# The last two rows of an output projection's weights loaded and multiplied in column halves, with the last half copied out of PSUM by two engines

## The chip, the cores and the metric

One core of one Trainium2 chip. The metric is the device time of one execution in microseconds (us), the median of several executions. The span of a profile is about 1.8 us shorter than the measured time of the same execution.

PE is TensorE, PEld its weight loads, DVE is VectorE, ACT is ScalarE, SP is SyncE. "q" after a name (SPq, ACTq) is that engine's sequencer, which issues DMAs. "Landing" is the moment when all 16 DMA engines that share a transfer have counted up its semaphore.

## The reference, cut to what matters

Grouped-query attention over a cache, followed by an output projection:

```
B, Sq, D = 32, 4, 1024;  Hq, Hkv, Sk, Dh = 32, 4, 2048, 128       # bf16
q = x @ wq ;  p = softmax(q k^T / sqrt(Dh)) ;  o = p v
y = o.transpose(0, 2, 1, 3).reshape(B, Sq, Hq * Dh) @ wo          # wo is (4096, 1024)
```

Only the last product matters here. `y` has 128 rows (batch times query) and 1024 columns. It is summed over 32 slices u of 128 values each; slice u needs one "row" of wo, 128 x 1024 values, 256 KB.

## The kernel before

The kernel streams 67 MB of K, 67 MB of V and the weights (151 MB in all) through one SyncE queue. The 8.4 MB of wo come last. They arrive in pieces of 4, 2 or 1 rows, the last row in two column halves; for each row PE runs two matmuls of 512 columns with the same weights, into two PSUM banks. The end of the kernel, with cuts marked:

```python
    WO = (4, 4, 4, 4, 4, 4, 2, 2, 2, 1)          # rows of wo for each piece
    NA = 512
    COLS = ((0, 0, NA), (NA, NA, D))              # (place in PSUM, first column, last column)
    # ...
        pieces = [(sum(WO[:c]), m, 0, D) for c, m in enumerate(WO)] + [(Hq - 1, 1, 0, NA), (Hq - 1, 1, NA, D)]
        # ... one DMA on SyncE's queue for each piece ...
        def oproj(u):
            for j, (at, n0, n1) in enumerate(COLS):
                # matmul for j == 0 (loads the weights), _matmul_held for the others (keeps them)
                p.op("pe", mm, [("wo", piece), ("ot", B - 1)], ("op", j) if u == Hq - 1 else None)

        def oproj_out():
            p.op("act", lambda e: e.activation(y_sb[:, 0:NA], ps_s[:, 0:NA], ACT.Copy), [("op", 0)], ("oe", 0))
            p.op("dve", lambda e: e.tensor_copy(y_sb[:, NA:D], ps_s[:, NA:D]), [("op", 1)], ("oe", 1))
            for j, (eng, n0, n1) in enumerate((("act", 0, NA), ("sp", NA, D))):
                p.dma(eng, ...out_flat[:, n0:n1]..., [("oe", j)], ("out", j), f"s_o{j}")
        # ...
        for u in range(Hq):
            oproj(u)
        oproj_out()
```

The pieces at the end are thus rows 28 and 29 together (512 KB), row 30 (256 KB), then 31a and 31b, the first and second half of row 31 (128 KB each).

## Time and profile before

| what | value |
|---|---|
| time, median of 3 runs | 363.42 us (363.31 to 363.45) |
| span of the profiled execution (363.58 us, not one of the three) | 361.8 us |
| mean DMA rate over the span | 419 GB/s |
| landings of the last four pieces | 356.81, 357.43, 357.78, 358.10 us |
| last output issued, landed, end | 359.515, 361.34, 361.79 us |

Two parts of the kernel before's page: the share of time in which the DMA engines were busy, in 40 slices of the span (a digit is tenths, 9 is 90% or more), and the chain of waits that ended last.

```profile
DMA  8999999999999999999999999999999999999995
...
## 4 chain that ended last, share of the span: by engine, by line
DMA 7%; PE 4%; SPq 0%; DVE 0%; issue 0%
```

The DMA row is full from the second slice to the last but one: the loads bound this kernel, and no engine's work in the middle is on the path. What this change can win is in the tail: from the last byte in to the end. The chain gives too coarse a view of that, so here is the timeline of the kernel before from 356.8 us: start, duration, engine, line, operation, output and inputs, and in brackets the idle time before and what ended it.

```profile
356.85 0.33 PEld L418 LDWEIGHTS ps_s<-big,KT_sb 128*128 128x128 bf16 x2 [0.91 <-DMA big<-in_wo_dram]
356.86 0.39 PE L418 MATMUL ps_s<-big,KT_sb 128*128 128x512 bf16 x1 [0.21 <-DMA big<-in_wo_dram]
357.08 0.38 PE L16 MATMUL ps_s<-big,KT_sb 128*128 128x512 bf16 x1
357.30 0.38 PE L418 MATMUL ps_s<-big,KT_sb 128*128 128x512 bf16 x1
357.52 0.38 PE L16 MATMUL ps_s<-big,KT_sb 128*128 128x512 bf16 x1
...
357.73 0.38 PE L418 MATMUL ps_s<-big,KT_sb 128*128 128x512 bf16 x1
357.95 0.38 PE L16 MATMUL ps_s<-big,KT_sb 128*128 128x512 bf16 x1
...
358.16 0.38 PE L418 MATMUL ps_s<-big,KT_sb 128*128 128x512 bf16 x1
358.38 0.38 PE L16 MATMUL ps_s<-big,KT_sb 128*128 128x512 bf16 x1
358.58 0.60 ACT L427 ACTIVATE P_sb<-ps_s 128x512 bf16<-128x512 f32 x1 [16.24 <-PE ps_s L418]
358.80 0.69 DVE L428 CAST P_sb<-ps_s 128x512 bf16<-128x512 f32 x1 [16.12 <-PE ps_s L16]
359.21 0.37 ACTq L430 DMA_DIRECT2D out_dram<-P_sb  x1
359.51 0.35 SPq L430 DMA_DIRECT2D out_dram<-P_sb  x1
```

Read it against the landings. PE waits for the 512 KB piece (landed 356.81), is let go at 356.86, and then runs eight matmuls one every 0.217 us without a gap. It is *behind* the loads: the last piece is there at 358.10, its matmul starts only at 358.38. After the last matmul VectorE copies 512 columns for 0.69 us, and only then is the second output issued. From the last landing to that issue, 1.42 us pass. ScalarE's copy and output, 0.2 us and more ahead, end nothing.

### The profile page before, as it was taken

The page shows a single profiled execution, that of the slowest core. Times are in us where ns is not written, and L with a number is a line of the kernel's source. Part 1 is how long each engine was busy: PE and PEld are TensorE (multiplying, and loading weights), DVE is VectorE, ACT ScalarE, POOL GpSimd, SP SyncE. Part 2 cuts the span into 40 slices and gives each one's busy share as a digit, 9 for nine tenths or more (in the row PEclk, how much of TensorE's full clock was granted, in tenths as well). Part 3 has the DMA queues.
Part 4 walks back from the last instruction along what each step waited for, and adds up shares of the span by engine and source line. Part 5 has one row for each costly group of instructions (what it writes and reads, how often), then busy time and mean ns, then how long its engine had stood idle before and what let it go on. Part 6 is the DMA issues. An engine that isn't in the chain of part 4 may idle for free. (4 is left out here: it accounts for less than half of the span.)

```text
span 361.8 us, 6210 instructions
## 1 busy us (share of the span) xinstructions
PE 307.2 (85%) x2998; PEld 146.8 (41%) x2338; DVE 269.1 (74%) x170; ACT 102.7 (28%) x110; POOL 165.3 (46%) x262
## 2 busy tenths in 40 slices
PE   1988788999989999988999888888888889889896
PEld 1002000454445544444445444444333344449711
DVE  0018799999899898879998888888888888856500
ACT  1014222333333333333333333333322223333000
POOL 8002055355555555554455444445555554444000
PEclk9999999999999999999999999999999999999999
DMA  8999999999999999999999999999999999999995
GB/s 328 429 431 433 429 428 420 431 428 428 425 422 435 426 429 424 432 428 431 426 424 435 425 431 424 429 431 429 429 424 431 429 429 424 428 433 428 412 414 197
DMA packets 11963, 151.66 MB, mean 419 GB/s; under 512 B 1328, under 2 KB 1840, under 8 KB 2480
## 3 DMA queue, kind: packets, MB, share of 16 engines
q1 hardware_dynamic: 11808, 151.39, 98.7%
q8 instruction: 6, 0.10, 0.1%
q10 hardware_dynamic: 144, 0.13, 0.1%
q14 instruction: 5, 0.04, 0.0%
HBM read 151.26 MB, written 0.26 MB: 419 GB/s over the span
## 5 line engine op out<-in xcount | busy, mean ns | idle before, releaser
L327 DVE STREAM_TRANSPOSE KT_sb<-big 128x2048 f32<-128x2048 f32 x64 | 146.6, 2293 | 16.8 <-DMA big<-in_k_cache_dram 16.8
L353 ACT ACTIVATE P_sb<-ps_s,negmx 128x2048 bf16<-128x2048 f32 x32 | 82.0, 2564 | 185.0 <-DVE negmx L349 185.0
L16 PE MATMUL ps_s<-KT_sb,QD_sb 128*128 128x512 bf16 x384 | 103.7, 377 | 0.0
L384 POOL COPY PD_sb<-PT_sb 32x1024 f32<-32x1024 f32 x62 | 64.1, 1034 | 63.4 <-PE ps_r L393 60.6
L384 POOL COPY big<-PT_sb 32x1024 f32<-32x1024 f32 x61 | 63.0, 1034 | 59.1 <-PE ps_r L393 56.3
L349 DVE TENSOR_REDUCE negmx<-ps_s 128x1 f32<-128x2048 f32 x32 | 73.2, 2286 | 12.4 <-PE ps_s L16 10.9
L393 PE MATMUL ps_r<-big 128*128 128x128 bf16 x1024 | 59.8, 219 | 11.3 <-PEq L85 11.3
L393 PE MATMUL ps_r<-big,PD_sb 128*128 128x128 bf16 x1024 | 59.8, 219 | 9.9 <-PEq L85 9.9
L393 PEld LDWEIGHTS ps_r<-big 128*128 128x128 bf16 x1024 | 57.9, 98 | 22.1 <-issue 21.6
L393 PEld LDWEIGHTS ps_r<-big,PD_sb 128*128 128x128 bf16 x1024 | 58.0, 98 | 21.2 <-issue 20.7
L340 PE MATMUL ps_s<-KT_sb,QD_sb 128*128 128x512 bf16 x128 | 48.3, 377 | 18.3 <-PEq L85 18.3
L340 PEld LDWEIGHTS ps_s<-KT_sb,QD_sb 128*128 128x128 bf16 x128 | 12.3, 96 | 103.1 <-issue 103.1
L362 DVE STREAM_TRANSPOSE PT_sb<-P_sb 128x1024 f32<-128x1024 f32 x32 | 39.8, 1245 | 15.8 <-ACT P_sb L353 15.8
L317 POOL COPY QD_sb<-QT_sb 32x64 f32<-32x64 f32 x128 | 29.4, 229 | 46.1 <-DVE QT_sb L296 20.4
L16 PE MATMUL ps_r<-ident 128*128 128x384 bf16 x173 | 33.3, 325 | 0.0
L365 PEld LDWEIGHTS ps_r<-ssum,permf 128*128 128x128 f32 x64 | 11.9, 187 | 24.8 <-issue 23.1
L402 ACT ACTIVATE QT_sb<-ps_r,rinv 128x128 bf16<-128x128 f32 x32 | 11.7, 367 | 29.5 <-PE ps_r L393 27.3
L278 DVE TENSOR_SCALAR KT_sb<-ps_r 128x512 bf16<-128x512 f32 x2 | 1.3, 686 | 20.1 <-PE ps_r L262 20.1
L16 PE MATMUL ps_s<-big,KT_sb 128*128 128x512 bf16 x32 | 12.1, 379 | 1.2 <-DVE KT_sb L409 1.1
L428 DVE CAST P_sb<-ps_s 128x512 bf16<-128x512 f32 x1 | 0.7, 691 | 16.1 <-PE ps_s L16 16.1
L418 PE MATMUL ps_s<-big,KT_sb 128*128 128x512 bf16 x30 | 11.4, 381 | 1.4 <-DMA big<-in_wo_dram 1.4
L251 PE MATMUL ps_r<-ident 128*128 128x384 bf16 x32 | 10.3, 322 | 0.0
(41 smaller groups left out, 85.3 us busy)
## 6 DMA issues: line engine op xcount, KB each, us to landing
big<-in_k_cache_dram SPq DMA_DIRECT2D x32, 2048.0 KB, 18.6
big<-in_v_cache_dram SPq DMA_DIRECT2D x32, 2048.0 KB, 22.1
big<-in_wq_dram SPq DMA_DIRECT2D x4, 2048.0 KB, 14.0
big<-in_wo_dram SPq DMA_DIRECT2D x6, 1024.0 KB, 22.8
big<-in_wo_dram SPq DMA_DIRECT2D x3, 512.0 KB, 24.5
P_sb<-in_x_dram SPq DMA_DIRECT2D x1, 256.0 KB, 2.7
big<-in_wo_dram SPq DMA_DIRECT2D x1, 256.0 KB, 21.8
big<-in_wo_dram SPq DMA_DIRECT2D x2, 128.0 KB, 19.1
```

Of the source, the lines that this page charges most:

```text
L16: return eng.add_instruction(mybir.InstMatmult(name=nc.get_next_instruction_name(), engine=eng.engine, start_tensor_calc=start, stop_tenso ...
L317: p.op("pool", lambda e, s=src, d=dst: e.tensor_copy(d, s), waits if g == 0 else [("pt", i - 2)] * (g == 1 and i > 1), ("qd", i) if g == G ...
L327: p.op("dve", lambda e, s=src, d=dst: e.transpose(d, s), waits, ("kt", i, c), gives="t_kt" if c else None)
L340: mm = lambda e, a_=(out_, lhsT, rhs), f=first, l=last: e.matmul(a_[0], lhsT=a_[1], rhs=a_[2], start=f, stop=l, skip_group_check=True)
L349: p.op("dve", lambda e: e.tensor_reduce(negmx[:, i % 4:i % 4 + 1], ps_s[:, :], AX.X, ALU.max, negate=True), [("qk", i)], ("negmx", i))
L353: p.op("act", lambda e: e.activation(P_sb[:, :, :, :].rearrange("p t r w -> p t w r"), ps_s[:, :].rearrange("p (t w r) -> p t w r", w=2, r=R),
L362: p.op("dve", lambda e: e.transpose(dst, src), [("exp", i)], ("pt", i))
L365: p.op("pe", lambda e: e.matmul(ring[(i if i == L else i // 2 * 2) % 4][:, 510 + i % 2:511 + i % 2], lhsT=permf[:, :], rhs=ssum[:, i % 4:i ...
L384: p.op("dve" if i >= B - 2 and g < i - B + 4 else "pool", lambda e, s=src, d=dst: e.tensor_copy(d, s), [free] * (g == 0 or i >= B - 2) + [ ...
L393: p.op("pe", lambda e: e.matmul(buf[:, 0:Dh], lhsT=pd_of(i)[:, t // 2, :, :, :, t % 2].rearrange("p x g q -> p (x g q)"), rhs=big[:, slot_ ...
L402: p.op("act", lambda e: e.activation(dst, src, ACT.Copy, scale=rinv[:, i % 4:i % 4 + 1]), [("pv", i), ("rinv", i)], ("o", i))
L418: mm = lambda e, a=(out_, lhsT, rhs): e.matmul(a[0], lhsT=a[1], rhs=a[2], start=(u == 0), stop=(u == Hq - 1), skip_group_check=True)
```

## The change

The intent is to shorten that stretch in three ways:

- **S** (split): rows 28 and 29 become two pieces, so that PE isn't held for both.
- **H** (halves): rows 30 and 31 land, and are multiplied, as 30a, 31a, 30b, 31b. The first half of y is finished before the second halves are in, and can be copied meanwhile.
- **C** (copies): the second half of y lies in two PSUM banks (288 and 224 columns), to be copied by ScalarE and VectorE at once. VectorE copies the first half too. Both outputs are issued on SyncE's queue.

Two banks are taken so that the two engines don't read the same one: the Trainium skill, "PSUM — Partial Sum Buffer", section "PSUM bank collisions raise a hardware error", says that two engines on one bank and quadrant at once raise an error and mostly read wrong data.

The diff, cut to its core:

```diff
-    WO = (4, 4, 4, 4, 4, 4, 2, 2, 2, 1)
+    WO = (4, 4, 4, 4, 4, 4, 2, 2, 1, 1)
     NA = 512
-    COLS = ((0, 0, NA), (NA, NA, D))
+    NB = 800
+    COLS = ((0, 0, NA), (512, NA, NB), (1024, NB, D))
...
-... + [(Hq - 1, 1, 0, NA), (Hq - 1, 1, NA, D)]
+... + [(Hq - 2, 1, 0, NA), (Hq - 1, 1, 0, NA), (Hq - 2, 1, NA, D), (Hq - 1, 1, NA, D)]
...
-            p.op("act", ...y_sb[:, 0:NA]..., [("op", 0)], ("oe", 0))
-            p.op("dve", ...y_sb[:, NA:D]..., [("op", 1)], ("oe", 1))
-            for j, (eng, n0, n1) in enumerate((("act", 0, NA), ("sp", NA, D))):
-                p.dma(eng, ..., [("oe", j)], ...)
+            for j, eng in enumerate(("dve", "act", "dve")):
+                copy(eng, *COLS[j], j)
+            for j, (n0, n1, waits) in enumerate(((0, NA, (0,)), (NA, D, (1, 2)))):
+                p.dma("sp", ..., [("oe", i) for i in waits], ...)
...
-        for u in range(Hq):
-            oproj(u)
+        for u in range(Hq - 2):
+            oproj(u, (0, 1, 2))
+        for js in ((0,), (1, 2)):
+            for u in (Hq - 2, Hq - 1):
+                oproj(u, js)
```

More of the change, by code (lines that the diff above doesn't have):

```diff
@@ L217, in bass_standalone__gqa_block_cached__sampling_kernel @@
         wo_v = wo.rearrange("(h p e) n -> p h (e n)", p=128, e=4)
-        pieces = [(sum(WO[:c]), m, 0, D) for c, m in enumerate(WO)] + [(Hq - 1, 1, 0, NA), (Hq - 1, 1, NA, D)]
-        assert sum(WO) == Hq - 1
+        pieces = [(sum(WO[:c]), m, 0, D) for c, m in enumerate(WO)] + [(Hq - 2, 1, 0, NA), (Hq - 1, 1, 0, NA), (Hq - 2, 1, NA, D), (Hq - 1, 1, NA, D)]
+        assert sum(WO) == Hq - 2
         for c, (u, m, n0, n1) in enumerate(pieces):
@@ L412, in oT_of, with oproj @@
             return oT_sb[:, u // 4, u % 4 // 2, :, :, u % 2].rearrange("p b s -> p (b s)")
-        def oproj(u):
-            for j, (at, n0, n1) in enumerate(COLS):
+        def oproj(u, js):
+            for j in js:
+                at, n0, n1 = COLS[j]
                 out_, lhsT, rhs = ps_s[:, at:at + n1 - n0], oT_of(u), wo_at(u, 1)[:, n0:n1]
-                if j == 0:
+                if j == js[0]:
                     mm = lambda e, a=(out_, lhsT, rhs): e.matmul(
@@ L426, in oproj_out, with copy @@
         def oproj_out():
-            p.op("act", lambda e: e.activation(y_sb[:, 0:NA], ps_s[:, 0:NA], ACT.Copy), [("op", 0)], ("oe", 0))
-            p.op("dve", lambda e: e.tensor_copy(y_sb[:, NA:D], ps_s[:, NA:D]), [("op", 1)], ("oe", 1))
-            for j, (eng, n0, n1) in enumerate((("act", 0, NA), ("sp", NA, D))):
-                p.dma(eng, lambda e, n0=n0, n1=n1: e.dma_start(out_flat[:, n0:n1], y_sb[:, n0:n1]),
-                      [("oe", j)], ("out", j), f"s_o{j}")
+            def copy(eng, at, n0, n1, j):
+                dst, src = y_sb[:, n0:n1], ps_s[:, at:at + n1 - n0]
+                if eng == "act":
+                    p.op(eng, lambda e: e.activation(dst, src, ACT.Copy), [("op", j)], ("oe", j))
+                else:
+                    p.op(eng, lambda e: e.tensor_copy(dst, src), [("op", j)], ("oe", j))
+            for j, eng in enumerate(("dve", "act", "dve")):
+                copy(eng, *COLS[j], j)
+            for j, (n0, n1, waits) in enumerate(((0, NA, (0,)), (NA, D, (1, 2)))):
+                p.dma("sp", lambda e, n0=n0, n1=n1: e.dma_start(out_flat[:, n0:n1], y_sb[:, n0:n1]),
+                      [("oe", i) for i in waits], ("out", j), f"s_o{j}")
         L = B - 1
```

## The prediction

> **What bounds the kernel now.** The loads: the page's DMA row is full in 38 of 40 slices, at a mean of 419 GB/s, and the chain of waits ends with wo loads and a short tail. The change touches only that tail; I read it from the timeline and the completion times of the loads.
>
> The last wo pieces complete at 356.81 us (rows 28 and 29, 512 KB), 357.43 (row 30), 357.78 (first half of row 31) and 358.10 (second half). Matmuls restart at 356.86 and run eight in a row, 0.217 us each, the last starting at 358.38. So PE, let go late by the 512 KB piece, ends 0.3 us later than the last data would force. ScalarE copies 512 columns (358.58, 0.60 us), VectorE the other 512 (358.80, 0.69 us). The last output issue starts at 359.51, its data lands at 361.34 (1.83 us later), and 0.45 us of closing work ends the span. From the last load to the last output issue: 1.41 us.
>
> **What the change does.**
> 1. Row 28 is there near 356.2 and row 29 near 356.85, so PE isn't held for both.
> 2. 30a, 31a, 30b, 31b land near 357.2, 357.5, 357.85, 358.17 (estimate). Bytes are the same; a 1 KB packet takes 46 ns against 84 ns for 2 KB, so row 30 in halves costs about 0.06 us.
> 3. The first half of y is finished after 31a, near 357.95: VectorE's 0.69 us copy runs 358.0 to 358.7, under the last loads and matmuls.
> 4. After 31b, matmuls of 288 and 224 columns start near 358.2 and 358.35 and end near 358.5 and 358.6. ScalarE: the Trainium skill, "ScalarE: Activation LUTs", section "What ACT_TABLE_LOAD costs", gives 186 ns plus 0.833 ns a column with immediate scale: 0.61 us for 512 (trace: 0.60), so an estimated 0.43 us for 288, to 358.95. VectorE: 0.69 us less 288 columns at 0.96 GHz ("VectorE: DVE Perf Modes", Specifications) is an estimated 0.39 us, from 358.7 (free of the first copy) to 359.1.
> 5. Both output issues are on SyncE, 0.35 us each: near 358.7 and 359.1. They don't collide.
> 6. A third matmul per row: 288 plus 224 columns stream as long as 512; PE's waits of 0.6 us at 350.5 and 353.0 absorb the rest. Two more load issues, made some 18 us before their landing, cost nothing.
>
> **Sum.** Last output issue from 359.51 to about 359.1: 0.4 us less, all on the critical path. Everything before 354 us is unchanged. Predicted 363.05 us, range 362.7 to 363.5; within 2% with 0.985, faster by over 2% 0.005, slower 0.01. The gain is 0.1%, above the spread of three runs (0.14 us).
>
> **What would show each step.** Timeline: PE's last waits are for the last halves; VectorE's first copy begins about 0.5 us before the last matmul ends; copies of about 0.43 and 0.39 us end near 358.95 and 359.1; second output issue near 359.1, landing 1.8 us later. The last load completes at 358.1 to 358.25.
>
> **What would make it wrong.** The last load landing after 358.3 (four small pieces with 1 KB rows); a longer landing of the second output, queued behind the first; a gap of over 0.1 us between VectorE's two copies; or slower restarts of PE when each half reloads its weights while data is awaited. Each is worth 0.1 to 0.3 us, so the gain could vanish, but not become 2%.

## The result, and the profile after

| | before | after |
|---|---|---|
| median of 6 runs | 363.43 us | 363.09 us |
| range of the 6 runs | 363.31 to 363.56 | 362.99 to 363.20 |
| ratio, 95% interval | | 0.9991 [0.9978, 1.0004] |

A ratio here is the mean time of one kernel's fast runs over the mean of the other's in the same rounds, so not quite the ratio of the medians quoted. At the 2% mark this is "the same". The interval just includes 1, but the two sets of six runs don't overlap, and a repetition below (five runs from 362.97 to 363.22 beside nine of before from 363.27 to 363.61) says the same: 0.34 us less by the medians here and 0.45 us there, about 0.1%.

The timeline of the kernel after, over the stretch shown above for before:

```profile
356.53 0.38 PE L420 MATMUL ps_s<-big,KT_sb 128*128 128x512 bf16 x1
356.74 0.38 PE L16 MATMUL ps_s<-big,KT_sb 128*128 128x288 bf16 x2
356.94 0.10 PEld L420 LDWEIGHTS ps_s<-big,KT_sb 128*128 128x128 bf16 x1 [0.41 <-DMA big<-in_wo_dram]
356.96 0.38 PE L420 MATMUL ps_s<-big,KT_sb 128*128 128x512 bf16 x1
...
357.40 0.84 PE L420 MATMUL ps_s<-big,KT_sb 128*128 128x512 bf16 x3
...
358.04 1.04 DVE L434 CAST P_sb<-ps_s 128x512 bf16<-128x512 f32 x2 [15.34 <-PE ps_s L420]
358.07 0.26 PE L16 MATMUL ps_s<-big,KT_sb 128*128 128x224 bf16 x1
358.25 0.10 PEld L420 LDWEIGHTS ps_s<-big,KT_sb 128*128 128x128 bf16 x1 [0.22 <-DMA big<-in_wo_dram]
358.26 0.30 PE L420 MATMUL ps_s<-big,KT_sb 128*128 128x288 bf16 x1
358.39 0.26 PE L16 MATMUL ps_s<-big,KT_sb 128*128 128x224 bf16 x1
358.59 0.41 ACT L432 ACTIVATE P_sb<-ps_s 128x288 bf16<-128x288 f32 x1 [16.23 <-PE ps_s L420]
358.76 0.82 SPq L439 DMA_DIRECT2D out_dram<-P_sb  x2
```

Instructions of the same line that follow each other are merged ("x2", named by the first one's shape). Singly, in the trace: VectorE copies 512 columns from 358.038 to 358.730 and 224 columns from 358.691 to 359.083; SyncE issues the two outputs at 358.757 and 359.225.

The landings of 28, 29, 30a, 31a, 30b, 31b are 356.24, 356.90, 357.21, 357.56, 357.89 and 358.21 us. PE is now level with the loads: it waits for 31a, 30b and 31b (30a's matmul still starts 0.19 us after its landing), and the last pair of matmuls starts at 358.26, 0.05 us after the last landing (before: 0.28 us). VectorE's long copy begins before that landing. The last issue is at 359.225 instead of 359.515, and its output lands at 360.96 instead of 361.34. From that landing to the end it is 0.45 us in both.

One point needs care. The *last load* doesn't land at the same time in each execution, and not in the order of the kernels: over the 14 traces it lies between 357.88 and 358.25 us. The spread is as large as the gain. So the experiments are judged by three distances inside one trace as well, which the loads' luck doesn't touch: from the last load's landing to the second output's issue, from that issue to its landing, and the sum of the two (the "tail").

### The profile page after: what moved, and what is told of

It reads as the page before. It is cut to its first block, busy times and chain, and to the rows that moved or that the text cites. A ratio compares the mean times of both kernels' runs of the same rounds, so it can differ in the third digit from the quotient of the medians.

```text
span 361.4 us, 6252 instructions
## 1 busy us (share of the span) xinstructions
PE 307.8 (85%) x3034; PEld 147.0 (41%) x2340; DVE 269.4 (75%) x171; ACT 102.6 (28%) x110; POOL 165.4 (46%) x262
## 5 line engine op out<-in xcount | busy, mean ns | idle before, releaser
L394 PE MATMUL ps_r<-big 128*128 128x128 bf16 x1024 | 59.8, 219 | 11.4 <-PEq L85 11.4
L420 PE MATMUL ps_s<-big,KT_sb 128*128 128x512 bf16 (+1 forms) x34 | 12.5, 375 | 2.0 <-DMA big<-in_wo_dram 1.2
L434 DVE CAST P_sb<-ps_s 128x512 bf16<-128x512 f32 (+1 forms) x2 | 1.0, 542 | 15.3 <-PE ps_s L420 15.3
L16 PE MATMUL ps_s<-big,KT_sb 128*128 128x224 bf16 (+1 forms) x62 | 12.0, 272 | 0.0
```

Source lines behind the costliest of these rows:

```text
L16: return eng.add_instruction(mybir.InstMatmult(name=nc.get_next_instruction_name(), engine=eng.engine, start_tensor_calc=start, stop_tenso ...
L394: p.op("pe", lambda e: e.matmul(buf[:, 0:Dh], lhsT=pd_of(i)[:, t // 2, :, :, :, t % 2].rearrange("p x g q -> p (x g q)"), rhs=big[:, slot_ ...
L420: mm = lambda e, a=(out_, lhsT, rhs): e.matmul(a[0], lhsT=a[1], rhs=a[2], start=(u == 0), stop=(u == Hq - 1), skip_group_check=True)
```

## The experiments

Twelve runs were made, in three sets of four, each set on one chip with its own runs of the kernel before. All gave correct results. Times are medians of five runs (before: three, after: six) beside the kernel before's of the same chip. Each distance is in us and from one trace; the column "last load to last copy's end" is part of the next one.

| run | parts | time (before, same chip) | last load | last load to last copy's end | last load to 2nd issue | 2nd issue to landing | tail |
|---|---|---|---|---|---|---|---|
| before | none | 363.42 | 358.10 | 1.39 | 1.42 | 1.82 | 3.24 |
| before_again | none | 363.34, one run (363.47) | 357.88 | 1.37 | 1.39 | 1.83 | 3.22 |
| s_only | S | 363.34 (363.53) | 357.98 | 1.17 | 1.20 | 1.82 | 3.02 |
| h_only | H | 363.43 (363.53) | 357.95 | 1.38 | 1.40 | 1.73 | 3.13 |
| c_only | C | 363.59 (363.53) | 358.00 | 1.45 | 1.65 | 1.73 | 3.38 |
| s_h | S, H | 363.25 (363.46) | 358.09 | 1.17 | 1.19 | 1.73 | 2.92 |
| s_c | S, C | 363.54 (363.46) | 357.93 | 1.25 | 1.45 | 1.74 | 3.19 |
| h_c | H, C | 363.39 (363.46) | 358.08 | 1.22 | 1.42 | 1.73 | 3.15 |
| after | S, H, C | 363.09 (363.43) | 358.21 | 0.87 | 1.01 | 1.74 | 2.75 |
| all_again | S, H, C | 363.08 (363.53) | 358.22 | 0.87 | 1.03 | 1.74 | 2.77 |
| waits | all, waits exchanged | 363.27 (363.46) | 358.25 | 0.87 | 1.03 | 1.75 | 2.78 |
| act_out | all, 1st output on ScalarE | 362.90 (363.47) | 357.94 | 0.87 | 0.97 | 1.73 | 2.70 |
| act_first | all, copies exchanged | 363.04 (363.47) | 358.09 | 0.84 | 0.93 | 1.73 | 2.65 |
| shared | all, both halves by both | 362.93 (363.47) | 358.08 | 0.84 | 0.91 | 1.71 | 2.61 |

The 95% intervals of the ratios are about 0.0013 (0.5 us) to either side, so the times alone tell few of these kernels apart; the distances in the traces do, and repeat within 0.025 us where a kernel was traced twice. Below, "before" and "after" without a run's name are the means of their two traces up to the second issue, 1.405 and 1.02 us.

My theory was that the three parts give the whole gain only together. Rival 1: the gain is PE's earlier release (S) and nothing else. Rival 2: the parts add up, and the shorter last copy (C) is the main one.

### s_only

```diff
-    WO = (4, 4, 4, 4, 4, 4, 2, 2, 2, 1)
+    WO = (4, 4, 4, 4, 4, 4, 2, 2, 1, 1, 1)
```

> The kernel before with one part of the change: rows 28 and 29 of wo as two pieces of 256 KB; row order, banks, copies and outputs as before. Theory (three parts that only work together): PE gets row 28 near 356.25 us and is level with the loads again, so the last matmul ends near 358.56 instead of 358.77; the VectorE copy of 512 columns still takes 0.69 us after it, so the last output issue starts near 359.31 instead of 359.51: 0.20 us faster. Rival 1 (the gain is PE's earlier release and nothing else): the whole 0.35 us. Rival 2 (the gain is the shorter last copy, each part counts for itself): 0.

Measured: 0.19 us faster by the medians, 0.21 us less from last load to second issue. The end of the timeline of the kernel with S alone:

```profile
357.82 0.38 PE L418 MATMUL ps_s<-big,KT_sb 128*128 128x512 bf16 x1
358.04 0.38 PE L16 MATMUL ps_s<-big,KT_sb 128*128 128x512 bf16 x1
358.24 0.60 ACT L427 ACTIVATE P_sb<-ps_s 128x512 bf16<-128x512 f32 x1 [16.06 <-PE ps_s L418]
358.46 0.69 DVE L428 CAST P_sb<-ps_s 128x512 bf16<-128x512 f32 x1 [15.94 <-PE ps_s L16]
```

The last matmul starts 0.06 us after the last landing (357.98). The copy behind it is unchanged. Rival 1 falls: the release is worth about half.

### h_only

```diff
 (to the kernel after)
-    WO = (4, 4, 4, 4, 4, 4, 2, 2, 1, 1)
+    WO = (4, 4, 4, 4, 4, 4, 2, 2, 2)
 (and columns, copies and outputs as before; matmuls of halves (0,) and (1,))
```

> The kernel before with one part of the change: rows 30 and 31 as first halves, then second halves, both in the loads and in the matmuls; rows 28 and 29 still one 512 KB piece, each half copied whole (ScalarE 0.60 us, VectorE 0.69 us), outputs on two queues. Theory: PE is let go at 356.86 by the 512 KB piece and has eight matmuls to run, the last ending near 358.75 whatever their order, so ScalarE's copy starts 0.2 us earlier, which ends nothing, and VectorE's ends near 359.5: 0.0 us of gain (between -0.05 and +0.05). Rival 1: 0. Rival 2 (parts add up): about 0.1 us faster.

Measured: 0.10 us faster by the medians, which is more than I expected, though within the noise of times. The issue is where it was expected (1.40 us after the last load, before: 1.42 and 1.39), so the order alone gains nothing up to there. The rest of the tail is 0.1 us shorter: the output lands 1.73 us after its issue instead of 1.82. This was the first sign of something the prediction hadn't: in this kernel the first output is issued 0.52 us ahead of the second instead of 0.31.

### c_only

```diff
 (to the kernel after)
-    WO = (4, 4, 4, 4, 4, 4, 2, 2, 1, 1)
+    WO = (4, 4, 4, 4, 4, 4, 2, 2, 2, 1)
 (and pieces as before)
-        for u in range(Hq - 2):
-            oproj(u, (0, 1, 2))
-        for js in ((0,), (1, 2)): ...
+        for u in range(Hq):
+            oproj(u, (0, 1, 2))
```

> The kernel before with one part of the change: second half in two banks, first half copied by VectorE, then 288 columns by ScalarE and 224 by VectorE, both outputs on one queue; loads and row order as before. Theory: the first half is finished only two matmuls before the end, near 358.54, so VectorE copies 512 columns from 358.58 to 359.27 and 224 columns only after that, to 359.64, and the second issue starts near 359.75: 0.15 to 0.25 us SLOWER than before. Rival 1: 0. Rival 2 (the shorter last copy is the gain): about 0.3 us faster.

Measured: 0.06 us slower by the medians, 0.24 us more from last load to second issue (expected 0.15 to 0.25). The end of the timeline of the kernel with C alone:

```profile
358.26 0.38 PE L16 MATMUL ps_s<-big,KT_sb 128*128 128x288 bf16 x2
358.46 0.99 DVE L434 CAST P_sb<-ps_s 128x512 bf16<-128x512 f32 x2 [15.79 <-PE ps_s L420]
358.58 0.41 ACT L432 ACTIVATE P_sb<-ps_s 128x288 bf16<-128x288 f32 x1 [16.25 <-PE ps_s L16]
359.18 0.82 SPq L439 DMA_DIRECT2D out_dram<-P_sb  x2
```

VectorE's two copies, 0.69 and 0.38 us, stand in a row, the first starting 0.47 us after the last landing (358.00): without H the first half is finished only two short matmuls before the second. ScalarE is done at 358.99 and idles. But the copies explain the smaller part of the loss: the second one ends 1.45 us after the last load, 0.08 us later than in before, and the second issue starts only 0.20 us after that (in before 0.03). Both outputs are on SyncE here, and the run `waits` takes this up. Rival 2 falls: C alone, as it was built, lengthens the path. The quicker landing (1.73 us) gives part of the loss back, again.

### all_again

The kernel after, unchanged.

> The whole change once more, on the same chip as the three parts. Both theories: 0.3 to 0.4 us faster than before, last load near 358.2, VectorE's copies near 358.04 to 359.08.

Measured: 0.45 us faster by the medians; last load to second issue 1.03 us, in the first trace 1.01. Beside it, the three parts measured alone on this chip give 0.21 less, nothing and 0.24 more up to the second issue, in sum no gain (0.03 us *more*); together they give 0.39 less. The parts don't add up.

### s_h

```diff
 (to the kernel after: columns, copies and outputs as before)
-    COLS = ((0, 0, NA), (512, NA, NB), (1024, NB, D))
+    COLS = ((0, 0, NA), (NA, NA, D))
-        for js in ((0,), (1, 2)):
+        for js in ((0,), (1,)):
```

> The whole change without its copies: rows 28 and 29 as two pieces and rows 30 and 31 in halves, but the second half in one bank, first half copied by ScalarE (0.60 us), second by VectorE (0.69 us), outputs on two queues. Theory: the last load lands near 358.2, its 512-column matmul ends near 358.65, VectorE copies from 358.68 to 359.37, last output issue near 359.39: about 0.12 us faster than before, less than the split alone, since the last load comes 0.1 us later. Rival 1 (PE's release alone): 0.35 us faster.

Measured: 0.21 us faster. Up to the issue it is what S alone gives (1.19 and 1.20 us): halves without the divided copy leave VectorE's 0.69 us behind the last matmul. I had expected the last load to be 0.1 us later than before; it landed at 358.09 here, inside the spread.

### s_c

```diff
 (to the kernel after: row 30 whole, row 31 in halves)
-    WO = (4, 4, 4, 4, 4, 4, 2, 2, 1, 1)
+    WO = (4, 4, 4, 4, 4, 4, 2, 2, 1, 1, 1)
 (and pieces and row order as before)
```

> The whole change without the half order: rows 28 and 29 as two pieces and the three copies, but row 30 whole, then row 31 in halves. Theory: the first half ends near 358.32, when 31a has been multiplied, so VectorE copies it from 358.35 to 359.04 and its 224 columns from there to 359.4; second issue near 359.53: 0.0 to 0.1 us faster than before. Rival 1: 0.35 us faster. Rival 2 (the shorter last copy): 0.3 us faster.

Measured: 0.08 us slower by the medians, which is outside what I had expected, though within the noise; 1.45 us from last load to second issue. In the timeline of this kernel VectorE's first copy starts 0.26 us after the last landing (357.93); with H it starts before it.

```profile
357.77 0.38 PE L420 MATMUL ps_s<-big,KT_sb 128*128 128x512 bf16 x1
357.99 0.38 PE L16 MATMUL ps_s<-big,KT_sb 128*128 128x288 bf16 x2
358.19 0.99 DVE L434 CAST P_sb<-ps_s 128x512 bf16<-128x512 f32 x2 [15.62 <-PE ps_s L420]
```

### h_c

```diff
 (to the kernel after)
-    WO = (4, 4, 4, 4, 4, 4, 2, 2, 1, 1)
+    WO = (4, 4, 4, 4, 4, 4, 2, 2, 2)
```

> The whole change with rows 28 and 29 as one 512 KB piece. Theory: PE is let go near 356.87, the first half ends near 358.34, VectorE copies it until 359.07 and its 224 columns until 359.42, second issue near 359.56: 0.0 to 0.1 us faster than before. Rival 1: 0. Rival 2: 0.3 us faster.

Measured: 0.07 us faster; 1.42 us from last load to second issue, 0.40 more than with S. PE, let go late, finishes the first half late: VectorE's first copy starts at 358.316, 0.23 us after the last landing, where with S it starts 0.16 to 0.18 us before it, and all that follows is later with it.

```profile
358.32 0.99 DVE L434 CAST P_sb<-ps_s 128x512 bf16<-128x512 f32 x2 [15.66 <-PE ps_s L420]
358.66 0.41 ACT L432 ACTIVATE P_sb<-ps_s 128x288 bf16<-128x288 f32 x1 [16.34 <-PE ps_s L420]
359.04 0.82 SPq L439 DMA_DIRECT2D out_dram<-P_sb  x2
```

So S is worth 0.21 us alone and 0.40 beside the others; H nothing alone and 0.43 beside the others; C costs 0.24 alone and gains 0.17 beside the others (all up to the second issue). The reason is one chain: last landing of a *first half*, its matmuls, VectorE's copy of 0.69 us, and then both issues on SyncE. In all six traces that have C with both outputs on SyncE and VectorE copying first (c_only, s_c, h_c, after, all_again, waits) the second issue starts 0.494 to 0.496 us after the end of that *first* copy, when the copy of 224 columns has been done for 0.14 to 0.20 us. So what counts is when the first copy starts: 0.23 to 0.47 us after the last landing where S or H is missing, 0.16 to 0.18 us before it where both are there.

C is two things, the divided copy (with VectorE on the first half too) and the move of both outputs to SyncE. Up to the end of the last copy C costs only 0.08 us alone and gains 0.30 beside the others; the rest, 0.17 alone and 0.13 beside them, is lost between the last copy and the second issue. No run has the divided copy with its outputs on two queues but without S or H, so how much of C's loss alone is the copies' is read from these distances and not from an experiment.

### waits

```diff
-            for j, (n0, n1, waits) in enumerate(((0, NA, (0,)), (NA, D, (1, 2)))):
+            for j, (n0, n1, waits) in enumerate(((0, NA, (0,)), (NA, D, (2, 1)))):
```

> The whole change with the two waits of the second output issue named in the other order. In the trace of after, VectorE's copy ends at 359.083, a wait instruction of SyncE on VectorE's semaphore is seen at 359.156, and the issue starts at 359.225, 0.142 us after the copy; in the kernel before, with one wait, it started 0.024 us after the copy. Theory: if the wait that comes last stands on the issue itself, the issue starts near 359.12 and 0.1 us more is gained (0.45 us faster than before). Rival: the 0.1 us is due to the two issues in a row on SyncE (the first ends at 359.104), and the order changes nothing.

Measured: 363.27 us (five runs from 362.99 to 363.61, wider than the others), and no change in the trace: last load to second issue 1.03 us (all_again: 1.03). SyncE's standalone wait is now on ScalarE's semaphore, whose copy was done at 359.041, and yet is seen only at 359.209, just after SyncE's first issue ended at 359.157; the second issue follows at 359.278. My reason falls, the rival holds. In all seven traces with both outputs on SyncE whose copies would have allowed an earlier issue or nearly so (c_only, s_c, h_c, after, all_again, waits and, at 0.487, act_first) the second issue starts 0.467 to 0.487 us after the first. In the first six it is 0.467 to 0.469, though the copies had been done for 0.14 to 0.20 us. Either order leaves one wait instruction between the two issues: 0.12 us lie between the end of the first (0.35 us long) and the start of the second, where each of the first loads of wo, with no such instruction between, starts 0.04 to 0.06 us after the end of the one before. So part of the distance may be that wait; no run has two outputs in a row without it.

### before_again

The kernel before, one look.

> The kernel before, for a second trace of it. How far do the loads move from one execution to the next, and does the second output again land 1.83 us after its issue? In all six traces of the runs so far with 0.47 us or more between the two output issues the second landed 1.73 to 1.74 us after its issue; with 0.31 us (before, and the split alone) 1.83 us. Theory (outputs issued close to each other hold each other up): 1.83 us again, since the issues are again 0.31 us apart. From the last load's completion to the last landing: 3.24 us, within 0.05. The last load's completion itself: 357.95 to 358.15.

Measured: tail 3.22 us, second output 1.83 us after its issue with the issues again 0.309 us apart, as expected; the last load was at 357.88, a little earlier than I had allowed. (The quoted text counts six traces with the longer distance; there were eight then, with 1.73 to 1.75 us.)

### act_out

```diff
-                p.dma("sp", lambda e, n0=n0, n1=n1: ...
+                p.dma(("act", "sp")[j], lambda e, n0=n0, n1=n1: ...
```

> The whole change with its first output issued on ScalarE's queue, after ScalarE's own copy. In all runs with two outputs on SyncE the second issue starts 0.468 us after the first, whether its data was ready 0.04 or 0.14 us before; so SyncE's pace, not the copy of 224 columns, is the last link. Theory: without the first issue in front of it the second starts near 359.11 to 359.16 (copy ends 359.08), some 0.08 us earlier, but the first output now starts near 359.03, and two outputs less than 0.31 us apart land slower (1.83 us instead of 1.73): 0.0 us of difference from the whole change, within 0.05. Rival (the landing was longer because of two queues, not of the short distance): also 1.83 us. Rival 2 (the landing differs only by chance): 1.73 us, 0.08 us faster than the whole change.

Measured: 362.90 us, 0.57 below before on that chip; tail 2.70 us, 0.05 to 0.07 below the kernel after's two traces. The end of this kernel's timeline:

```profile
357.76 1.05 DVE L434 CAST P_sb<-ps_s 128x512 bf16<-128x512 f32 x2 [15.21 <-PE ps_s L420]
...
358.33 0.41 ACT L432 ACTIVATE P_sb<-ps_s 128x288 bf16<-128x288 f32 x1 [16.11 <-PE ps_s L420]
358.48 0.37 ACTq L439 DMA_DIRECT2D out_dram<-P_sb  x1
358.91 0.35 SPq L439 DMA_DIRECT2D out_dram<-P_sb  x1
```

(The quoted text has data ready 0.04 us before an issue; the traces show 0.14 to 0.20.) My expectation was wrong in one premise: I had put ScalarE's issue behind the end of its own copy. The trace shows the issue at 358.48 in the middle of the copy (358.33 to 358.74), as soon as VectorE's first copy was done. That agrees with the Trainium skill, "PSUM — Partial Sum Buffer", section "Engine vs sequencer instructions": the sequencer waits for earlier instructions to be dispatched, not to complete. So the two issues are 0.43 us apart, and the second output lands after 1.73 us although there are two queues. With h_only and s_h (also two queues, 1.73 us at 0.52 and 0.75 us apart) this rules out "two queues" as the reason for 1.82. Chance is ruled out as well: three traces at 0.309 us apart show 1.824 to 1.829, eleven at 0.427 and more show 1.707 to 1.753. That fits outputs holding each other up when close, but *why* is not shown; no run sets the distance alone. In the three close traces the second issue also starts 0.06 us before the first has ended, in the eleven others after its end, so the overlap of the issues is as good a candidate as the distance.

The second issue is 0.05 us nearer to the last load, all that freedom from SyncE's pace brings: it still starts 0.096 us after the last copy, with SyncE's wait instruction seen 0.03 us after that copy and the issue 0.07 us behind the wait (before, with one wait, 0.03 us in all). So the second wait seems to cost a little once the pace is out of the way. The small gain fits what the Trainium skill, "DMA: Bandwidth & Descriptors", section "Issuing engines are not separate DMA queues", says: issuing from several engines saves the sequencer's time only.

### act_first

```diff
-            for j, eng in enumerate(("dve", "act", "dve")):
+            for j, eng in enumerate(("act", "dve", "act")):
```

> The whole change with ScalarE and VectorE exchanged: ScalarE copies the first half (0.60 instead of 0.69 us), VectorE 288 columns and ScalarE 224 of the second. Theory: first copy from 358.04 to 358.64, first issue near 358.67, so SyncE may issue again from 359.14; VectorE 358.60 to 359.06, ScalarE 358.69 to 359.05; second issue near 359.14, landing 1.73 us later: from last load to last landing 2.66 us instead of 2.75, time 0.05 to 0.1 us below the whole change. Rival (the last copy is the last link, not SyncE's pace): 0.02 us.

Measured: tail 2.65 us, as expected (2.66); time 0.43 us below before, so not told apart from the kernel after by time. Here the copies end at 358.929 and 358.924 and the second issue starts at 359.017, 0.487 us after the first: the two limits have nearly met.

### shared

```diff
-    COLS = ((0, 0, NA), (512, NA, NB), (1024, NB, D))
+    NC = 256
+    COLS = ((0, 0, NC), (1536, NC, NA), (512, NA, NB), (1024, NB, D))
-            for j, eng in enumerate(("dve", "act", "dve")):
+            for j, eng in enumerate(("dve", "act", "dve", "act")):
 (outputs wait for copies 0 and 1, and for 2 and 3; four matmuls per row)
```

> The whole change with the first half in two banks too, 256 columns each: VectorE copies 256, then 288 columns, ScalarE 256, then 224; four matmuls per row. Theory: first copies end near 358.4, first issue near 358.5, second copies end near 359.06, second issue near 359.12 (now bound by the copies, no longer by SyncE), landing 1.73 us later: from last load to last landing about 2.65 us, some 0.1 us below the whole change. It must not lose time in the four matmuls per row, which stream the same 1024 columns.

Measured: 362.93 us, 0.54 below before; tail 2.61 us, the shortest of all. The end of its timeline:

```profile
358.26 0.26 PE L16 MATMUL ps_s<-big,KT_sb 128*128 128x224 bf16 x1
358.39 0.94 SPq L440 DMA_DIRECT2D out_dram<-P_sb  x2
358.46 0.46 DVE L435 CAST P_sb<-ps_s 128x288 bf16<-128x288 f32 x1 [0.23 <-PE ps_s L421]
358.56 0.36 ACT L433 ACTIVATE P_sb<-ps_s 128x224 bf16<-128x224 f32 x1 [0.26 <-PE ps_s L16]
```

The first issue begins before the last copies do, and both engines now wait for PE, not for themselves (the brackets name PE, with idle time before). The path is now: landing, two matmuls, one short copy on each engine, one issue. By time, the ranges of act_out and shared (362.87 to 362.95, and 362.89 to 363.12) lie below all runs of before on their chip (363.32 to 363.56); by the 2% mark both are still "the same". That they beat the kernel after is shown by the tails (0.05 to 0.15 us) and not by times, which come from different chips with last loads up to 0.3 us apart.

## Why the prediction was right, point by point

- **Bound by loads, only the tail moves.** Right. The spans differ by 0.38 us, and so do the landings of the last output; PE's waits for loads up to 353 us are the same (a 0.6 us wait ends at 353.02 before and 353.04 after).
- **Step 1, PE's release.** Right: rows 28 and 29 land at 356.24 and 356.90 (predicted 356.2 and 356.85). s_only shows 0.21 us for it, of the 0.3 us of lag that the prediction named.
- **Step 2, the halves' landings.** 357.21, 357.56, 357.89, 358.21 against 357.2, 357.5, 357.85, 358.17. That small packets cost 0.06 us is neither shown nor refuted: the last load lands at 358.10 on the mean of the nine traces with four halves and at 357.98 on that of the five others, which is the expected direction, but the ranges overlap and the spread over executions, 0.37 us, is larger.
- **Step 3, the first copy under the last loads.** Right, within 0.04 us (358.04 to 358.73), and by the runs with one or two of the parts the heart of the gain.
- **Step 4, sizes of the last copies.** ScalarE 288 columns 0.412 us (predicted 0.43), VectorE 224 columns 0.392 us (0.39), ending at 359.01 and 359.08 (358.95 and 359.1). The Trainium skill's formula for ScalarE was good within 0.02 us.
- **Step 5, "They don't collide".** Wrong. The first issue, at 358.757, ends at 359.104, and SyncE starts its next one 0.468 us after the first's start, at 359.225 rather than 359.1. The last link is SyncE's pace, led by the *first* copy, and not the copy of 224 columns, which was done 0.14 us earlier. The runs waits and act_out show it: exchanging the waits changes nothing, and taking the first issue off SyncE brings the second 0.05 us nearer.
- **Landing, "1.8 us later".** Off by 0.09 us to the other side: 1.74 us. I took the duration from the kernel before, where the other output had been issued 0.31 us earlier. The prediction had named a *longer* landing behind the first output as a risk; it became shorter.
- **Step 6, costs of a third matmul and two more issues.** Right in the cost: 288 and 224 columns stream in the time of 512 (c_only: 0.219 us for the pair, 0.216 for 512). Wrong in "some 18 us before their landing": the last two issues took 6.3 and 2.1 us and started 17.4 and 11.4 us before their landing, which was still early enough.
- **The sum.** 0.4 us, where the medians show 0.34 and the traces 0.38. The two errors after the copies, 0.12 and 0.09 us, have opposite signs and nearly cancel; that is luck, and the total was better than its terms. That it was the *parts together* that mattered, and that C by itself would lose time, the prediction did not say, but the same arithmetic gave it for the experiments.

## What to carry to other kernels

In a load-bound kernel, write down for its last pieces when each lands, when its matmul starts, when its copy starts and when its output is issued: what is done before the last landing cost nothing here, the rest was paid. Dividing the last copy paid only where the engine that gets the piece was free by then, so finish, copy and issue an earlier part of the result under the last loads; test such parts together, since here one alone gave half the gain, one nothing, and one did harm. When outputs follow each other closely on one engine, count the distance of its issues (0.47 us here, with a wait between) as a stage of its own.

## What the Trainium skill lacked or had wrong

- "DMA: Bandwidth & Descriptors" gives no distance from one issue to the next on a queue, with a wait between them, for this chip. Here SyncE's second output issue starts 0.467 to 0.469 us after the first in six traces, with the issue itself 0.347 us long and a wait instruction between them.
- The same page has no landing time for stores that follow each other closely. 128 KB stores landed 1.82 to 1.83 us after their issue when another such store had been issued 0.31 us before (three traces), and 1.71 to 1.75 us with 0.43 us or more (eleven traces). The cause is open.
- The same page doesn't say how long an issue takes when many others are queued. In the kernel after, the first seven issues of wo took 0.33 to 0.43 us, the seven behind them 1.15, 3.30, 2.09, 2.13, 0.45, 6.28 and 2.13 us. What held them is not shown.
- The same page (Specifications) gives 512 B as the minimum transfer for line rate. Here the step isn't as sharp: packets of 1 KB took 46 ns and of 2 KB 84 ns (medians, last stretch of the kernel before), about a tenth more time per byte.
- No page says what instruction fetches do to a stream of loads on the same DMA engines ("Runtime: NRT & Kernel Launch", section "Instruction fetch mechanics", would be the place). In all 14 traces the 16 DMA engines finish the loads that land at 47 and 52 us within 0.3 to 0.7 us of each other, and 1.5 to 2.0 us apart soon after the first 16 KB instruction packet, a single packet of 1.02 us. In three traces that packet came near 64.5 instead of 56 us, and the step moved with it, from the load landing at 58 to 59 us to that landing at 68 to 69. At the end of the kernel after, the first engine is done with the last piece at 356.33 us and the last one at 358.21. The two come together in 14 of 14 traces, but no experiment shows that one causes the other. Those 1.9 us are five times what the change gained.
